# Attention feeding a two-level mixture of experts on one core: split weight loads, gate products moved to the end of a phase, and a rearranged start

## The chip, the cores and the metric

The kernel runs on one core of a Trainium2 chip. A core has five engines that run side by side[...]: TensorE (PE in the profile, with its weight loads as PEld) multiplies matrices, VectorE (DVE) and ScalarE (ACT) work on elements, GpSimd (POOL) [...]issues some of the transfers, SyncE (SP) issues the rest. TensorE writes its products to PSUM[...]. The metric is the device time of one execution in microseconds; lower is better.

## What is computed

Eight batches of multi-query attention (16 heads share one key and value head, 384 tokens, head size 64) are followed by a mixture of experts: 4 groups of 4 experts, each expert being two products of 1024 by 1024 with a ReLU between.

```python
scores = (q @ k.T) / 8                       # q: 8 x 16 x 384 x 64; k, v: 8 x 1 x 384 x 64
attn = softmax(scores)                       # over the keys
x = (attn @ v) -> (3072 tokens, 1024)        # heads side by side
g_idx = argmax(x @ w_group)                  # 4 groups
e_idx = argmax(x @ w_expert[g_idx])          # 4 experts in the group
combined = softmax weight of the group * softmax weight of the expert
out = combined * (relu(x @ w1[g_idx, e_idx]) @ w2[g_idx, e_idx])
```

All values are float32; w1 and w2 are 4 MB each for each of the 16 experts.

## The kernel before

It works through 24 *pieces* `p`, three pieces of 128 tokens for each batch. For one piece, `scores(p, j)` makes the scores of all heads against 64 keys (j = 0 to 5) and their exponentials; `pre_add`, `fold_keys`, `join` and `invert` build the sums over keys and their inverse; `values(p - 1, j)` multiplies the exponentials of the piece *before* by v; `weigh(p - 1)` divides and writes the result to `xT` (float32) on VectorE and to `xbf` (bf16) on GpSimd.

Most tokens of a batch choose the same expert, so the kernel counts the choices of the first 128 tokens of a batch, takes the most frequent expert, loads its two weight matrices and applies it to the whole batch. Pairs of a batch and an expert that this misses are done at the end. The work of one batch is 14 *units*: 8 `h_unit`s (first product and ReLU) and 6 `y_unit`s (second product). They are put into *phases* behind the attention of a piece, four or five at a time, so that TensorE always has work.

```python
def load_w1(w1, e):                       # two transfers, each with all 1024 columns of F
    for a in range(2):
        nc.gpsimd.dma_start(out=w1[a * D:(a + 1) * D], in_=w1f[bass.ds(e, 1), a]...)

def choose_b(b):                          # counts of the first 128 tokens, then the weight loads
    ps = side([P, GE], FP32, "c1ps")
    nc.tensor.matmul(out=ps[:], lhsT=ones_bf[:], rhs=first[b]..., start=True, stop=True)
    cnt = pool.tile([P, GE], FP32, tag="cnt1", bufs=1, name="cnt1")
    nc.vector.tensor_copy(out=cnt[:], in_=ps[:])
    nc.vector.max_with_indices(out_max=top[:], out_indices=idx[:], in_=cnt[:])
    reg = nc.values_load(idx[0:1, 0:1], engines=(ET.Pool,), ...)
    load_w1(w1, reg)
    nc.gpsimd.dma_start(out=w2[:], in_=w2f[bass.ds(reg, 1)]...)

def gate_c(b):                            # counts of the whole batch, and gsel, the y_units' scale
    ps = side([P, ST, GE], FP32, "cps")
    nc.tensor.matmul(out=ps[:]..., lhsT=ones_bf[:], rhs=ohe_t[b]..., start=True, stop=True)
    nc.vector.reduce_sum(out=cnt[:], in_=ps[:].rearrange("p s e -> p e s"), axis=AX)
    ...                                   # five more small VectorE operations, the last one writes gsel

def phase(n, jobs):
    for i in range(n):
        fill(1)                           # one unit, if the weights of its batch have been asked for
        some_q()                          # one transfer of a later q
        if i > 0 and jobs:
            jobs.pop(0)()
    while jobs:
        jobs.pop(0)()

def jobs_gates(b):                        # in the phase of each batch's second piece
    return [gate_a of b, gate_both(b), count_both(b)]     # cut: for b = 0 three smaller ones

FIVES = (9, 13, 17, 20)
for p in range(NP):
    b, st = divmod(p, ST)
    for j in range(3):
        scores(p, j)
    if p == 0:   prep_k(1)
    elif p == 1: turn_q(2, ...)           # q of piece 2 turned by TensorE, copied by ScalarE
    elif p == 2: turn_q(3, ...)
    elif p < NP - 1: prep_q(p + 1)        # q of the next piece turned by VectorE
    for j in range(KB):                   # KB = 6
        if jobs: jobs.pop(0)()
        if p > 0: values(p - 1, j)
        if j == 2 and p > 0: join(p - 1)
        if j + 3 < KB: scores(p, j + 3)
        if j > 0: pre_add(p, j)
        if j == 2 and p > 0: invert(p - 1)
        if j == 3: stats_q(p)
        ...
    if p > 0: weigh(p - 1)
    fold_keys(p)
    ...
    if p >= ST:                           # from piece 3 on
        phase(5 if p in FIVES else 4, jobs)
```

`gate_a` is the product of `xT` with the gate weights (ScalarE copies it to `part`), `gate_both` sums it up and lets VectorE find the maxima (`choose_a`, `gate_logits`, `gate_math`; its result `ohe` is the operand of the count products), `count_both` is `choose_b` and `gate_c`. All products but those of `values` rotate through three PSUM slots of two banks (`ps_s`, tag "s"); `values` has one slot of its own. The exponentials have nine buffers, `presum` one. Before the loop, q of pieces 0 and 1 are turned by TensorE. After the loop, the last units run between the small steps that find and do the pairs left over.

Of the kernel before, what the change touches and what calls it, by code (L numbers as in the profile page):

```python
# [9 lines left out]
FP32 = mybir.dt.float32  # L10
# [3 lines left out]
P = 128  # L14
ACTF = mybir.ActivationFunctionType
OP = mybir.AluOpType
AX = mybir.AxisListType.X
# [4 lines left out]
def kernel(  # L22
# [11 lines left out]
    nc = tc.nc  # L34
    B, H, S, D = q.shape
# [37 lines left out]
    def side(shape, dtype, name):  # L73
        return ps_s.tile(shape, dtype, tag="s", name=name)
# [20 lines left out]
    def some_q(n=1):  # L95
        for _ in range(n):
            if q_todo:
                q_todo.pop(0)()
# [38 lines left out]
            q_nat.append(qe)  # L137

    def load_w1(w1, e):
        for a in range(2):  # L140
            nc.gpsimd.dma_start(out=w1[a * D:(a + 1) * D], in_=w1f[bass.ds(e, 1), a].rearrange("e p k f -> (e p) k f"))  # L141

    ones_bf = singles.tile([P, P], BF16, name="ones_bf")
    nc.vector.memset(ones_bf[:], 1.0)
# [72 lines left out]
    def turn_q(p, nat, copies):  # L217
        qT[p] = pool.tile([P, 2 * CW], FP32, tag="qT", bufs=2, name="qT")
        n = HP // len(copies)
        for i, copy in enumerate(copies):  # L220
            ps = side([P, 2 * CW], FP32, "qps")
            for h in range(n):
                nc.tensor.transpose(out=ps[:, h * P:(h + 1) * P], in_=nat(i * n + h).rearrange("p a d -> p (a d)"), identity=ident[:])
            copy(out=qT[p][:, i * n * P:(i + 1) * n * P], in_=ps[:, 0:n * P])
# [78 lines left out]
    def gate_a(b, lo, hi):  # L303
        n = (hi - lo) * P
        ps = side([P, CW], FP32, "gps")
        for r in range(2):
            for j in range(4):
                ko = 4 * r + j
                nc.tensor.matmul(out=ps[32 * j:32 * j + 32, 0:n], lhsT=gw[:, ko, :], rhs=xT[b][:, ko, lo * P:hi * P], start=(r == 0), stop=(r == 1), tile_position=(0, 32 * j))
        part[b] = part_all  # L310
        nc.scalar.copy(out=part[b][:, lo * P:hi * P], in_=ps[:, 0:n])

    def gate_b(b, lo=0, hi=ST):
        ps = side([P, ST, 32], FP32, "lps")
        for st in range(lo, hi):
            nc.tensor.matmul(out=ps[:, st, :], lhsT=part[b][:, st * P:(st + 1) * P], rhs=sel[:], start=True, stop=True)  # L316
        return ps
# [3 lines left out]
    def choose_a(b, ps):  # L321
        gate_logits(b, ps, 0, 1)
        L = logits[b][:, 0]
        mx = pool.tile([P, 5], FP32, tag="mx1", bufs=1, name="mx1")
        nc.vector.reduce_max(out=mx[:], in_=L, axis=AX)
        oh = pool.tile([P, 5, 4], FP32, tag="oh1", bufs=1, name="oh1")
        nc.vector.tensor_tensor(out=oh[:], in0=L, in1=mx[:].unsqueeze(2).to_broadcast([P, 5, 4]), op=OP.is_ge)
        ohe = pool.tile([P, 4, 4], BF16, tag="ohe1", bufs=1, name="ohe1")
        nc.vector.tensor_mul(out=ohe[:], in0=oh[:, 1:5, :], in1=oh[:, 0, :].unsqueeze(2).to_broadcast([P, 4, 4]))
        first[b] = ohe  # L330

    def choose_b(b):
        ps = side([P, GE], FP32, "c1ps")
        nc.tensor.matmul(out=ps[:], lhsT=ones_bf[:], rhs=first[b][:].rearrange("p g e -> p (g e)"), start=True, stop=True)
        cnt = pool.tile([P, GE], FP32, tag="cnt1", bufs=1, name="cnt1")
        nc.vector.tensor_copy(out=cnt[:], in_=ps[:])
        top = pool.tile([P, 8], FP32, tag="top", bufs=1, name="top")
        idx = pool.tile([P, 8], U32, tag="idx", bufs=2, name="idx")
        nc.vector.max_with_indices(out_max=top[:], out_indices=idx[:], in_=cnt[:])
        reg = nc.values_load(idx[0:1, 0:1], engines=(ET.Pool,), min_val=0, max_val=GE - 1, skip_runtime_bounds_check_because="an index into 16 counts")  # L340
        w1 = wpool.tile([P, KO, F], BF16, tag="w1", name="w1")
        load_w1(w1, reg)
        w2 = wpool.tile([P, FO, Dm], BF16, tag="w2", name="w2")
        nc.gpsimd.dma_start(out=w2[:], in_=w2f[bass.ds(reg, 1)].rearrange("a p k f -> (a p) k f"))
        wts[b] = (w1, w2)
        choice[b] = idx
# [26 lines left out]
        gv = gate_all[:, b * GE:(b + 1) * GE, :].rearrange("p (g e) s -> p s g e", g=G)  # L373
        nc.vector.tensor_mul(out=gv, in0=ohe[:], in1=tt[:].unsqueeze(3).to_broadcast([P, ST, 4, 4]))

    def gate_c(b):
        ps = side([P, ST, GE], FP32, "cps")
        nc.tensor.matmul(out=ps[:].rearrange("p s e -> p (s e)"), lhsT=ones_bf[:], rhs=ohe_t[b][:].rearrange("p s g e -> p (s g e)"), start=True, stop=True)
        cnt = pool.tile([P, GE], FP32, tag="cnt", bufs=1, name="cnt")
        nc.vector.reduce_sum(out=cnt[:], in_=ps[:].rearrange("p s e -> p e s"), axis=AX)  # L380
        idf = pool.tile([P, 1], FP32, tag="idf", bufs=1, name="idf")
        nc.vector.tensor_copy(out=idf[:], in_=choice[b][:, 0:1])
        mask = pool.tile([P, GE], FP32, tag="mask", bufs=1, name="mask")
        nc.vector.tensor_scalar(out=mask[:], in0=iota16[:], scalar1=idf[:, 0:1], scalar2=None, op0=OP.is_equal)
        nc.vector.scalar_tensor_tensor(out=extra[:, b * GE:(b + 1) * GE], in0=cnt[:], scalar=0.0, in1=mask[:], op0=OP.is_gt, op1=OP.subtract)
        gm = pool.tile([P, ST, GE], FP32, tag="gm", bufs=1, name="gm")
        nc.vector.tensor_mul(out=gm[:], in0=gate_all[:, b * GE:(b + 1) * GE, :].rearrange("p e s -> p s e"), in1=mask[:].unsqueeze(1).to_broadcast([P, ST, GE]))
        gs = pool.tile([P, ST], FP32, tag="gsel", bufs=4, name="gsel")
        nc.vector.reduce_sum(out=gs[:], in_=gm[:], axis=AX)  # L389
        gsel[b] = gs  # L390
# [47 lines left out]
    stats_k(0)  # L438
    turn_k_first()
    turn_q(0, lambda h: q_raw[0][:, 0, h], [nc.scalar.copy, nc.vector.tensor_copy])  # L440
    turn_q(1, lambda h: q_raw[0][:, 1, h], [nc.vector.tensor_copy])
    load_gw()

    units = []
# [2 lines left out]
    def fill(n):  # L447
        while n > 0:
            if not units:
                if begun[0] >= B or begun[0] not in wts:  # L450
                    return
                units.extend(first_units(begun[0]))
                begun[0] += 1
            units.pop(0)()
            n -= 1

    def phase(n, jobs):
        for i in range(n):
            fill(1)
            some_q()  # L460
            if i > 0 and jobs:
                jobs.pop(0)()
        while jobs:
            jobs.pop(0)()

    def gate_both(b):
        ps = gate_b(b)
        choose_a(b, ps)
        gate_logits(b - 1, ps, 1, ST)
        gate_math(b - 1)  # L470

    def count_both(b):
        choose_b(b)
        gate_c(b - 1)

    def jobs_gates(b):
        if b == 0:
            return [lambda: gate_a(0, 0, 1), lambda: choose_a(0, gate_b(0, 0, 1)), lambda: choose_b(0)]
        return [lambda: gate_a(b, 0, ST), lambda: gate_both(b), lambda: count_both(b)]

    bound = {}
    oki = singles.tile([1, 1], I32, name="oki")
# [17 lines left out]
        nc.vector.tensor_copy(out=oki[:], in_=okf[:])  # L500
        bound["okf"] = okf

    FIVES = (9, 13, 17, 20)
    for p in range(NP):
        b, st = divmod(p, ST)
        jobs = jobs_gates(0) if p == 2 else []
        if st == 0 and b + 1 < B:
            load_q(b + 1)
        for j in range(3):
            scores(p, j)  # L510
        if p == 0:
            prep_k(1)
        elif p == 1:
            turn_q(2, lambda h: q_raw[0][:, 2, h], [nc.scalar.copy])
        elif p == 2:
            turn_q(3, lambda h: q_nat[h // HC][:, h % HC], [nc.scalar.copy])
        elif p < NP - 1:
            prep_q(p + 1)
        for j in range(KB):
            if jobs:  # L520
                jobs.pop(0)()
            if p > 0:
                values(p - 1, j)
            if j == 2 and p > 0:
                join(p - 1)
            if j + 3 < KB:
                scores(p, j + 3)
            if j > 0:
                pre_add(p, j)
            if j == 2 and p > 0:  # L530
                invert(p - 1)
            if j == 3:
                stats_q(p)
            if p < 4 and 0 < j < 5:
                some_q()
        assert not jobs
        if p > 0:
            weigh(p - 1)
        fold_keys(p)
        if st == 1 and b + 1 < B:  # L540
            if b > 0:
                load_k(b + 1)
            load_v(b + 1)
        if st == 2 and b + 1 < B:
            if b > 0:
                prep_k(b + 1)
            stats_k(b + 1)
        if p >= ST:
            jobs = []
            if st == 1:  # L550
                jobs = jobs_gates(b)
            if p == NP - 1:
                jobs = [bound_a, bound_b]
            phase(5 if p in FIVES else 4, jobs)

    done[0] = True
    join(NP - 1)
# [8 lines left out]
    gate_logits(last, gate_b(last, 1, ST), 1, ST)  # L566
    gate_math(last)
    fill(1)
    gate_c(last)
    fill(1)  # L570
    pe = side([P, CW], FP32, "pe")
    nc.tensor.matmul(out=pe[:, 0:1], lhsT=extra[0:1, :], rhs=one[0:1, 0:1], start=True, stop=True)
# [238 lines left out]
```

## Time and profile before

| What | Value |
|---|---|
| Time, median of three executions | 493.03 us (492.92 to 494.19) |
| Span of the profiled execution | 491.4 us |
| Mean granted TensorE clock | 0.993 |
| DVE busy | 307.9 us (63%) |
| ACT busy | 247.8 us (50%) |
| POOL busy | 48.0 us (10%) |
| Exponentials on ACT (144) | 142.1 us |
| Score products on PE | 141.9 us |
| Value products on PE | 140.6 us |
| First and second expert products on PE | 90.9 and 86.7 us |
| Weights of one batch: two transfers for w1, one for w2 | 12.9 and 23.9 us to landing |

Busy times of different engines overlap and do not add up to the span. In the timeline each line is a run of like instructions with its start and length; the bracket gives the idle time of that engine just before it, and what is taken to have ended it. A wait for several semaphores is put down to the last one that the profile shows, so the name in the bracket is at times that of an engine which had long been done.

### The profile page before, as it was taken

Reading aid. Unit: us, or ns where it says so; the run is one execution under the profiler, and the core shown is the slowest. Engines: PE = TensorE matmul, PEld = TensorE weight load, DVE = VectorE, ACT = ScalarE, POOL = GpSimd, SP = SyncE. Lnnn points to the kernel's source line nnn. Section 1 sums busy time; section 2 is a strip of 40 time slices with the busy share of each in tenths; the row PEclk is TensorE's granted clock in tenths of the full one; section 3 lists DMA queues with packets and bytes.
Section 4 is the critical chain, followed back from the end, with each engine's and each line's share of the span. In section 5 each row is a group of like instructions: output and inputs, shape, how many; then the busy total and the mean of one; then the engine's idle time right before and its main releaser. Section 6 shows DMA issues by size and latency. Waiting matters only on the chain. (4 is left out here: it accounts for less than half of the span.)

```text
span 491.4 us, 9357 instructions
## 1 busy us (share of the span) xinstructions
PE 466.2 (95%) x3828; PEld 202.7 (41%) x3828; DVE 307.9 (63%) x487; ACT 247.8 (50%) x346; POOL 48.0 (10%) x64
## 2 busy tenths in 40 slices
PE   7999698999999998999999999999999999999993
PEld 6333244333344334434434334433434434445651
DVE  4779737856777847866677756855686675734200
ACT  2966263664456463565456464565465455423231
POOL 1002000200010000200010002000010002001000
PEclk9999899999999999999999999999999999999998
DMA  8797992996949595996789386977599303985990
GB/s 161 93 118 130 218 187 36 158 245 169 126 66 213 135 222 65 154 211 175 129 119 208 106 187 114 192 146 187 120 155 209 119 21 102 200 190 150 238 261 29
DMA packets 146242, 74.52 MB, mean 152 GB/s; under 512 B 120443, under 2 KB 120443, under 8 KB 146192
## 3 DMA queue, kind: packets, MB, share of 16 engines
q0 software_dynamic: 19008, 37.84, 42.6%
q1 hardware_dynamic: 126384, 35.81, 36.0%
q8 instruction: 32, 0.52, 0.4%
q10 hardware_dynamic: 800, 0.20, 0.2%
q14 instruction: 18, 0.15, 0.1%
HBM read 92.62 MB, written 19.40 MB: 228 GB/s over the span
## 5 line engine op out<-in xcount | busy, mean ns | idle before, releaser
L248 ACT ACTIVATE pt<-s 128x1024 f32<-128x1024 f32 x144 | 142.1, 1026 | 69.7 <-PE s L246 68.5
L246 PE MATMUL s<-qT,kT 64*64 64x512 f32 x1152 | 141.9, 595 | 2.3 <-ACT hT L402 1.7
L285 PE MATMUL o<-pt,v 64*64 64x512 f32 x1152 | 140.6, 590 | 1.2 <-DVE xT L296 1.2
L256 DVE TENSOR_TENSOR presum<-presum,pt 128x1024 f32<-128x1024 f32 x96 | 116.6, 1215 | 7.9 <-DVE presum L254 0.5
L401 PE MATMUL hps<-xbf,w 128*128 128x384 bf16 x512 | 90.9, 330 | 5.4 <-POOL xbf L297 5.0
L409 PE MATMUL yps<-w,hT 128*128 128x512 bf16 x384 | 86.7, 379 | 0.0
L285 PEld LDWEIGHTS o<-pt,v 64*64 64x64 f32 x1152 | 43.4, 133 | 78.7 <-issue 74.9
L401 PEld LDWEIGHTS <-w 128*128 128x128 bf16 x512 | 49.1, 100 | 50.3 <-issue 21.5
L254 DVE TENSOR_TENSOR presum<-pt 128x1024 f32<-128x1024 f32 x24 | 29.1, 1214 | 61.2 <-ACT pt L248 61.1
L402 ACT ACTIVATE hT<-hps 128x384 bf16<-128x384 f32 x64 | 31.3, 489 | 71.2 <-PE hps L401 71.1
L246 PEld LDWEIGHTS s<-qT,kT 64*64 64x64 f32 x1152 | 39.8, 133 | 63.6 <-issue 51.4
L297 POOL CAST xbf<-xT 128x1024 bf16<-128x1024 f32 x24 | 25.0, 1042 | 332.9 <-DVE xT L296 332.9
L409 PEld LDWEIGHTS <-hT 128*128 128x128 bf16 x384 | 36.3, 98 | 49.3 <-issue 8.9
L410 ACT ACTIVATE y<-yps,gsel 128x512 f32<-128x512 f32 x36 | 24.8, 688 | 48.9 <-PE yps L409 41.8
L296 DVE TENSOR_TENSOR xT<-o,rinv 128x1024 f32<-128x1024 f32 x24 | 29.2, 1218 | 3.6 <-PE o L285 3.6
L275 DVE STREAM_TRANSPOSE rinv<-rc 128x1024 f32<-128x1024 f32 x24 | 29.9, 1246 | 0.8
L260 DVE TRANSPOSE_TENSOR_REDUCE fold<-presum 128x32 f32<-128x1024 f32 x24 | 29.6, 1235 | 0.0
L273 DVE RECIPROCAL rc<-sm 128x32 f32<-128x32 f32 x24 | 8.6, 358 | 29.6 <-PE sm L268 29.5
L238 DVE STREAM_TRANSPOSE qT<-qraw 128x1024 f32<-128x1024 f32 x20 | 24.3, 1215 | 2.0 <-DMA qraw<-in_q_dram 1.7
L204 ACT ACTIVATE junk<-qraw 128x1024 bf16<-128x1024 f32 x21 | 22.0, 1049 | 0.0
L141 POOL DMA_DIRECT2D w<-in_moe_w_dram x18 | 12.6, 706 | 69.8 <-DVE gsel L389 43.5
L351 DVE COPY L<-lps 128x20 f32<-128x20 f32 (+1 forms) x16 | 3.0, 186 | 25.5 <-PE lps L316 25.5
(147 smaller groups left out, 187.9 us busy)
## 6 DMA issues: line engine op xcount, KB each, us to landing
w<-in_moe_w_dram POOLq DMA_DIRECT2D x18, 1024.0 KB, 12.9
w<-in_moe_w_dram POOLq DMA_DIRECT2D x9, 2048.0 KB, 23.9
qraw<-in_q_dram SPq DMA_DIRECT2D x56, 192.0 KB, 5.0
out_dram<-y SPq DMA_DIRECT2D x36, 256.0 KB, 4.4
x_bf<-xbf SPq DMA_DIRECT2D x8, 768.0 KB, 3.7
out_dram<-yt SPq DMA_DIRECT2D x12, 256.0 KB, 6.1
v<-in_v_dram SPq DMA_DIRECT2D x16, 96.0 KB, 2.6
k<-in_k_dram SPq DMA_DIRECT2D x28, 48.0 KB, 3.3
```

The lines of the kernel that those rows point to most:

```text
L246: nc.tensor.matmul(out=ps[64 * c:64 * c + 64, a, :], lhsT=kT[b][r, j * D:(j + 1) * D], rhs=qT[p][r, c * CW:(c + 1) * CW], start=True, stop ...
L248: nc.scalar.activation(out=t[:], in_=ps[:], func=ACTF.Exp, scale=scale)
L254: nc.vector.tensor_add(out=presum[p][:], in0=pt[p, 0][:], in1=pt[p, 1][:])
L256: nc.vector.tensor_add(out=presum[p][:], in0=presum[p][:], in1=pt[p, j][:])
L260: nc.vector.tensor_reduce(out=fold[p][:], in_=presum[p][:].rearrange("p a (n i) -> p (a n) i", i=32), axis=AX, op=OP.add, apply_transpose= ...
L275: nc.vector.transpose(out=t[:].rearrange("p (b i) -> p b i", i=32), in_=rc[:].rearrange("p c b -> p (c b)").unsqueeze(2).to_broadcast([P, ...
L285: nc.tensor.matmul(out=o_ps[p][64 * a:64 * a + 64, c, :], lhsT=v_sb[b][r, j, :], rhs=pt[p, j][r, a, :], start=(j == 0), stop=(j == KB - 1))
L296: nc.vector.tensor_mul(out=xT[b][:, :, ts], in0=o_ps[p][:].rearrange("p c (h n) -> p (c h) n", n=P), in1=rinv[p][:].rearrange("p (h n) -> ...
L297: nc.gpsimd.tensor_copy(out=xbf[b][:, :, ts], in_=xT[b][:, :, ts])
L401: nc.tensor.matmul(out=ps[:, 0:S], lhsT=w1[:, ko, fc * P:(fc + 1) * P], rhs=xb[:, ko, :], start=(ko == 0), stop=(ko == KO - 1))
L402: nc.scalar.activation(out=state["h"][:, fc, :], in_=ps[:, 0:S], func=ACTF.Relu)
L409: nc.tensor.matmul(out=ps[:], lhsT=state["h"][:, fo, st * P:(st + 1) * P], rhs=w2[:, fo, nh * CW:(nh + 1) * CW], start=(fo == 0), stop=(fo ...
```

## The change

The change reorders work and splits transfers; the products computed stay the same.

1. **Weights by halves of F.** w1 is loaded in four transfers instead of two, the first 512 columns first, so that the first four `h_unit`s need only the first half.
2. **Start.** The turn of q for piece 1 goes behind the first scores of piece 0. The turns for pieces 2 and 3 move from before the values loop of pieces 1 and 2 to its fourth step.
3. **Sums earlier.** `pre_add` for j = 1 and 2 stands ahead of the values loop, the others at j = 1 to 3 instead of 3 to 5.
4. **First units inside block 4.** The phase of piece 3 is dropped. Piece 4 does three units between its first three scores and the values of piece 3. `FIVES` is rearranged; the number of units by the end of the loop stays 88.
5. **Gate products last in a phase.** `gate_a` stands behind the last but one unit of a phase, `gate_both` behind the last one.
6. **Counts together.** The two count products go one piece later, into one PSUM slot; ScalarE copies both with one instruction, and VectorE reads the copy.

```diff
     def load_w1(w1, e):
-        for a in range(2):
-            nc.gpsimd.dma_start(out=w1[a * D:(a + 1) * D], in_=w1f[bass.ds(e, 1), a]...)
+        for c in range(2):
+            fs = slice(c * F // 2, (c + 1) * F // 2)
+            for a in range(2):
+                nc.gpsimd.dma_start(out=w1[a * D:(a + 1) * D, :, fs], in_=w1f[bass.ds(e, 1), a, :, :, fs]...)
...
+    def counts(now, full):
+        n = GE * (1 + ST)
+        ps = side([P, n], FP32, "cps")
+        lo, hi = (0 if now is not None else GE), (n if full is not None else GE)
+        ...                                  # one product for `now`, one for `full`
+        t = pool.tile([P, n], FP32, tag="cnt1", bufs=1, name="cnt1")
+        nc.scalar.copy(out=t[:, lo:hi], in_=ps[:, lo:hi])
+        ...                                  # choose_b(now, t[:, 0:GE]); gate_c(full, t[:, GE:n])
...
     turn_q(0, ...)
-    turn_q(1, ...)
...
-        return [lambda: gate_a(b, 0, ST), lambda: gate_both(b), lambda: count_both(b)]
+        return [lambda: gate_a(b, 0, ST), lambda: gate_both(b)]
...
-    FIVES = (9, 13, 17, 20)
+    FIVES = (8, 12, 16, 20, 22)
...
         for j in range(3):
             scores(p, j)
+            if p == 0 and j == 0:
+                turn_q(1, ...)
         if p == 0:
             prep_k(1)
-        elif p == 1:
-            turn_q(2, ...)
-        elif p == 2:
-            turn_q(3, ...)
-        elif p < NP - 1:
+        elif 2 < p < NP - 1:
             prep_q(p + 1)
+        if jobs:
+            jobs.pop(0)()
+        if p == ST + 1:
+            fill(3)
+        for j in (1, 2):
+            pre_add(p, j)
         for j in range(KB):
-            if jobs:
-                jobs.pop(0)()
             if p > 0:
                 values(p - 1, j)
...
-            if j > 0:
-                pre_add(p, j)
+            if 0 < j < 4:
+                pre_add(p, j + 2)
             if j == 2 and p > 0:
                 invert(p - 1)
             if j == 3:
                 stats_q(p)
+                if p == 1:
+                    turn_q(2, ...)
+                elif p == 2:
+                    turn_q(3, ...)
+            if jobs:
+                jobs.pop(0)()
...
-        if p >= ST:
-            jobs = []
+        if p > ST:
+            n = 5 if p in FIVES else 4
+            steps = {}
+            if st == 2 and b > 0:
+                steps = {0 if b == 1 else 1: lambda: counts(b, b - 1)}
             if st == 1:
-                jobs = jobs_gates(b)
+                gate_a_, gate_b_ = jobs_gates(b)
+                steps = {n - 2: gate_a_, n - 1: gate_b_}
+                if b == B - 1:
+                    steps = {1: gate_a_, 2: gate_b_, n - 1: lambda: counts(b, b - 1)}
             if p == NP - 1:
-                jobs = [bound_a, bound_b]
-            phase(5 if p in FIVES else 4, jobs)
+                steps = {1: bound_a, 2: bound_b}
+            for i in range(n):
+                fill(1)
+                some_q()
+                if i in steps:
+                    steps[i]()
...
-    gate_c(last)
+    counts(None, last)
```

More of the change, by code (lines that the diff above doesn't have):

```diff
@@ L139, in load_w1 @@
     def load_w1(w1, e):
-        for a in range(2):
-            nc.gpsimd.dma_start(out=w1[a * D:(a + 1) * D], in_=w1f[bass.ds(e, 1), a].rearrange("e p k f -> (e p) k f"))
+        for c in range(2):
+            fs = slice(c * F // 2, (c + 1) * F // 2)
+            for a in range(2):
+                nc.gpsimd.dma_start(out=w1[a * D:(a + 1) * D, :, fs], in_=w1f[bass.ds(e, 1), a, :, :, fs].rearrange("e p k f -> (e p) k f"))
     ones_bf = singles.tile([P, P], BF16, name="ones_bf")
@@ L330, in choose_a, with choose_b @@
         first[b] = ohe
[L332 to L336, printed above, removed]
+    def counts(now, full):
+        n = GE * (1 + ST)
+        ps = side([P, n], FP32, "cps")
+        lo, hi = (0 if now is not None else GE), (n if full is not None else GE)
+        if now is not None:
+            nc.tensor.matmul(out=ps[:, 0:GE], lhsT=ones_bf[:], rhs=first[now][:].rearrange("p g e -> p (g e)"), start=True, stop=True)
+        if full is not None:
+            nc.tensor.matmul(out=ps[:, GE:n], lhsT=ones_bf[:], rhs=ohe_t[full][:].rearrange("p s g e -> p (s g e)"), start=True, stop=True)
+        t = pool.tile([P, n], FP32, tag="cnt1", bufs=1, name="cnt1")
+        nc.scalar.copy(out=t[:, lo:hi], in_=ps[:, lo:hi])
+        if now is not None:
+            choose_b(now, t[:, 0:GE])
+        if full is not None:
+            gate_c(full, t[:, GE:n])
+    def choose_b(b, cnt):
         top = pool.tile([P, 8], FP32, tag="top", bufs=1, name="top")
         idx = pool.tile([P, 8], U32, tag="idx", bufs=2, name="idx")
-        nc.vector.max_with_indices(out_max=top[:], out_indices=idx[:], in_=cnt[:])
+        nc.vector.max_with_indices(out_max=top[:], out_indices=idx[:], in_=cnt)
         reg = nc.values_load(idx[0:1, 0:1], engines=(ET.Pool,), min_val=0, max_val=GE - 1, skip_runtime_bounds_check_because="an index into 16 counts")
@@ L374, in gate_math, with gate_c @@
         nc.vector.tensor_mul(out=gv, in0=ohe[:], in1=tt[:].unsqueeze(3).to_broadcast([P, ST, 4, 4]))
-    def gate_c(b):
-        ps = side([P, ST, GE], FP32, "cps")
-        nc.tensor.matmul(out=ps[:].rearrange("p s e -> p (s e)"), lhsT=ones_bf[:], rhs=ohe_t[b][:].rearrange("p s g e -> p (s g e)"), start=True, stop=True)
+    def gate_c(b, per):
         cnt = pool.tile([P, GE], FP32, tag="cnt", bufs=1, name="cnt")
-        nc.vector.reduce_sum(out=cnt[:], in_=ps[:].rearrange("p s e -> p e s"), axis=AX)
+        nc.vector.reduce_sum(out=cnt[:], in_=per.rearrange("p (s e) -> p e s", s=ST), axis=AX)
         idf = pool.tile([P, 1], FP32, tag="idf", bufs=1, name="idf")
@@ L440 @@
     turn_q(0, lambda h: q_raw[0][:, 0, h], [nc.scalar.copy, nc.vector.tensor_copy])
-    turn_q(1, lambda h: q_raw[0][:, 1, h], [nc.vector.tensor_copy])
     load_gw()
@@ L455, in fill @@
             n -= 1
[L457 to L461, printed above, removed]
-                jobs.pop(0)()
-        while jobs:
-            jobs.pop(0)()
     def gate_both(b):
@@ L470, in gate_both @@
         gate_math(b - 1)
-    def count_both(b):
-        choose_b(b)
-        gate_c(b - 1)
     def jobs_gates(b):
         if b == 0:
-            return [lambda: gate_a(0, 0, 1), lambda: choose_a(0, gate_b(0, 0, 1)), lambda: choose_b(0)]
-        return [lambda: gate_a(b, 0, ST), lambda: gate_both(b), lambda: count_both(b)]
+            return [lambda: gate_a(0, 0, 1), lambda: choose_a(0, gate_b(0, 0, 1)), lambda: counts(0, None)]
+        return [lambda: gate_a(b, 0, ST), lambda: gate_both(b)]
     bound = {}
@@ L510 @@
             scores(p, j)
+            if p == 0 and j == 0:
+                turn_q(1, lambda h: q_raw[0][:, 1, h], [nc.vector.tensor_copy])
         if p == 0:
             prep_k(1)
-        elif p == 1:
-            turn_q(2, lambda h: q_raw[0][:, 2, h], [nc.scalar.copy])
-        elif p == 2:
-            turn_q(3, lambda h: q_nat[h // HC][:, h % HC], [nc.scalar.copy])
-        elif p < NP - 1:
-            prep_q(p + 1)
+        elif 2 < p < NP - 1:
+            prep_q(p + 1)
+        if jobs:
[4 more added lines that the diff above has]
+            pre_add(p, j)
         for j in range(KB):
-            if jobs:
-                jobs.pop(0)()
             if p > 0:
@@ L533 @@
                 stats_q(p)
-            if p < 4 and 0 < j < 5:
+                if p == 1:
+                    turn_q(2, lambda h: q_raw[0][:, 2, h], [nc.scalar.copy])
+                elif p == 2:
+                    turn_q(3, lambda h: q_nat[h // HC][:, h % HC], [nc.scalar.copy])
+            if jobs:
+                jobs.pop(0)()
+            if p <= ST and 0 < j < 5:
                 some_q()
```

## The prediction, made before the changed kernel ran

> **What bounds the kernel now.** I read the busy times of the page first, then TensorE's waits, then the timelines around each wait.
>
> ```profile
> PE 466.2 (95%) x3828; PEld 202.7 (41%) x3828; DVE 307.9 (63%) x487; ACT 247.8 (50%) x346; POOL 48.0 (10%) x64
> ```
>
> TensorE is busy for 466.2 of 491.4 us, and the change takes no product away. So only its idle 25 us, and products that ran at a lower clock, can be won. Of the 25, about 8 lie behind the last product at 483.6 us, 1.3 ahead of the first.
>
> ```profile
> PE hps L401 <- POOL xbf L297: 5.0, 2, 4.3
> PE cps L378 <- DVE ohe L365: 2.8, 6, 0.5
> PE s L246 <- ACT hT L402: 1.7, 5, 0.3
> PE gps L309 <- ACT hT L402: 1.7, 3, 0.6
> PE qps L223 <- DMA qn<-in_q_dram: 1.2, 1, 1.2
> PE o L285 <- DVE xT L296: 1.2, 1, 1.2
> PE qps L223 <- ACT pt L248: 0.8, 1, 0.8
> PE s L246 <- ACT y L410: 0.6, 1, 0.6
> PE pq L493 <- DVE sq L487: 0.5, 1, 0.5
> ```
>
> Columns: total us, times, longest. With 0.3 more for hps these waits are 15.8; reading every idle stretch over 0.1 us off the timeline I get 16.0. They fall in two kinds. Up to 66 us: 1.19 at 8.0, 0.80 at 18.2, 1.19 at 43.6, 4.29 at 52.8, together 7.47. After it: the gates, once a batch, and two single ones, together 8.5. TensorE's timeline shows one of each kind:
>
> ```profile
> 57.12 7.04 PE L401 MATMUL hps<-xbf,w 128*128 128x384 bf16 x32 [4.29 <-POOL xbf L297]
> ...
> 74.67 2.77 PE L401 MATMUL hps<-xbf,w 128*128 128x384 bf16 x16
> 78.01 1.50 PE L309 MATMUL gps<-xT,gw 128*32 128x384 f32 x16 [0.57 <-ACT hT L402]
> ...
> 83.28 0.20 PE L378 MATMUL cps<-ohe,ones_bf 128*128 128x48 bf16 x1 [0.47 <-DVE ohe L365]
> 83.82 2.81 PE L246 MATMUL s<-qT,kT 64*64 64x512 f32 x24 [0.35 <-ACT hT L402]
> ```
>
> The first line holds a second loss: 32 products took 7.04 us, 16 of the same took 2.77, so some 1.5 us went to a lower clock after the idle stretch. The windows view (PE, PEld, DVE, ACT, POOL, granted clock, DMA) has it as 0.76:
>
> ```profile
> 57.00:64.20 7.20, 7.08 (x36) 3.68 (x39) 1.24 (x2) 1.48 (x4) 0.07 (x1) 0.76 1.27 207
> ```
>
> What is behind the 4.29 us is VectorE. Its timeline:
>
> ```profile
> 50.98 3.84 DVE L256 TENSOR_TENSOR presum<-presum,pt 128x1024 f32<-128x1024 f32 x3
> 54.74 1.22 DVE L296 TENSOR_TENSOR xT<-o,rinv 128x1024 f32<-128x1024 f32 x1
> 55.88 1.24 DVE L260 TRANSPOSE_TENSOR_REDUCE fold<-presum 128x32 f32<-128x1024 f32 x1
> ```
>
> The values of piece 2 were ready at 52.8, but VectorE still added exponentials until 54.7, then weighed, and GpSimd's cast to bf16 ran from 56.02 to 57.06. The first unit started at 57.12. The weights were not the cause: w1's second half of partitions landed at 52.7 by the semaphore's times. The same lag of VectorE is at the second kind: weigh(3) ran 76.65 to 77.9, and gate_a, put down to ACT, started at 78.01.
>
> [...] The trace has no w1 split by columns; it shows the transfers of one batch following each other[...].
>
> **The start (parts 2, 3, 4).** Scores of piece 0 need only the first turn, copied at about 8.8. They start near 8.3 and wait for the second copy, the second turn follows at 9.3 when its q has landed. First scores then end near 9.4 rather than 11.2, but the exponential for j = 1, which VectorE's first add waits for, comes only behind the turn: it ends near 12.3 against 13.3. From there VectorE has no pause in my walk. Adds are 1.27 us apart, invert 1.56, weigh 1.13, fold 1.2, prep_q 1.13, the gate steps of batch 0 together 1.4 with waits (all start to start in its timeline). Piece 0: 5 adds and fold, 7.8, to 20.1. Piece 1: 5 adds, invert, weigh, fold, 10.2, to 30.3. Piece 2: the same and the gate steps, 11.7, to 42.0. Piece 3: prep_q, 5 adds, invert, weigh, 10.2, to 52.2. Cast: 53.3, against 57.06.
>
> TensorE in the same walk: piece 1 ends near 26.4, piece 2 near 39.5 (before, 40.8), scores of piece 3 to 42.1, no wait for weigh(1), which ends at 40.9; values of piece 2 end at 50.2 against 52.83. Scores of piece 4 need nothing new and go to 52.7. A wait of 0.6 for the cast, under the length that lowered the clock, then three units at 1.35 until 57.4. Before, with four units, the same point was 64.09 + 2.63 = 66.7; a fourth unit at 1.35 makes it 65.4 at like work. **Gain 8.0**, which is 7.47 + 1.5 less about 1.0 of small new waits.
>
> **The weights (part 1).** choose_b comes some 1.9 us earlier; four columns-by-partition quarters land at about 5.5 us for each half. First columns are there near 45, well ahead of 53. On POOL four issues of 0.69 take 1.4 us more a batch, beside everything. In the steady part the load starts a piece later, about 14 us after the old moment, but the units of that batch begin 22 us or more after that. Worth by itself: 0 to 0.3 us.
>
> **The gates (parts 3, 5, 6).** Walking one piece from the start of its scores: joins come at 7.2, so before, invert at 7.2 pushed three adds behind it and weigh ended at 13.7; now only the last add is behind it, and weigh ends near 12.3, with values ending at 10.4. gate_a stands two units later still, so 0.57 goes. Counts are asked for a piece after ohe exists, so 0.47 goes, and 0.35 ahead of the scores with them. The stretches for batches 1 to 7 are 1.39, 1.37, 1.39, 0.96, 0.81, 0.80, 0.58: 7.3 us. The others are 0.73 at 115.6 (a unit waiting for xbf) and 0.48 (bound_b behind a late VectorE); both get the 1.4 us of an earlier weigh. **Gain 8.5 at most.** The counts' copy on ACT costs 8 times about 0.2 us on an engine that is half idle: nothing.
>
> **What I take off.** gate_both right ahead of the scores makes ACT wait for dl (about 1.6 us) before the next exponential; that one then ends 2.9 us after gate_b, and its slot is needed at 3.5. Margins of half a us will not all hold. At the end, the last w2 landed at 478.0 and its products began at 479.98; the split w1 goes ahead of it in the queue, and 2 us of room may shrink to 1. I take 1.5 us off for these. Sum: 8.0 + 8.5 - 1.5 = 15.0, so 493.0 - 15.0 = **478.0 us**.
>
> **The rivals.**
> First, *the wait moves*: VectorE, busy 11.65 of 12.0 us up to 57, remains the limit at the start, and any pause in it (a late exponential, the count's copy now behind two exponentials on ACT) goes straight into the cast. For it speaks that my walk leaves it no slack; against it, that a delay of the cast by 2 us costs just 2. If the start gives 5 instead of 8[...]: 482 to 483.
> Second, *gates merely displaced*: the chain part, gate_b, dl, ex now stands against the next exponentials, and VectorE starts its adds 3 us later in each third piece; kT of the next batch is then done near 32.9 on a clock where its scores start at 33.9. If 0.7 us a batch returns: 483.
> Third, *transfers*: 2 KB rows instead of 4 KB and loads that overlap other q transfers; q took 20.9 us to land beside the weights at 36 to 64 us. If the end waits for w2, or a prep_q for q: 2 to 4 us, 480 to 482.
>
> **Range and chances.** Each alone leaves a gain over 2% (under 483.2) or just at it; two together lose it. The most that can be won is 16.0 + 1.5, 475.5. So the range is 475.5 to 483.5, faster by over 2% at 0.87, within 2% at 0.11, slower 0.02, the last for a stall that I do not see at all.
>
> **What would show it.** Right: no stretch over 1 us ahead of the first unit, that unit near 53, clock 1.0 throughout to the end; no wait of cps on ohe nor of gate_a; VectorE without pause from 12 to 52. Wrong: hps waiting for xbf by 2 us or more, scores waiting in each third piece for an exponential or for kT, py waiting for the last weights, or PE busy time itself changed.

## The result and the profile after

The changed kernel takes 497.16 us (median of four, 495.48 to 497.63) against 492.98 in the same comparison: 1.0074 times as long, 95% interval 1.0045 to 1.0103. A gain of 15 us was predicted; it lost 4.

The page's busy line, and then the waits of TensorE (line, what it waited for, total us, times, longest), of the changed kernel:

```profile
PE 467.5 (94%) x3810; PEld 203.9 (41%) x3828; DVE 304.4 (61%) x479; ACT 248.0 (50%) x355; POOL 60.3 (12%) x82
```

```profile
PE s L248 <- DVE top L352: 12.0, 4, 4.6
PE s L248 <- ACT y L421: 3.9, 2, 2.9
...
PE hps L412 <- POOL xbf L299: 0.6, 1, 0.6
```

The old waits are gone: cps on ohe, gps on VectorE's weigh, 4.3 us on xbf (now 0.6). New ones stand in their place. The scores wait 12.0 us in four places, put down to `top`, VectorE's maximum of the counts. `top` is no operand of the scores. What VectorE does just ahead of it is `kT` of the next batch, which is. VectorE's timeline around the longest of the four, in the third piece of batch 3:

```profile
186.32 0.22 DVE L387 TENSOR_TENSOR gate_all<-ohe,tt 128x48 f32<-128x48 bf16 x1
193.11 1.25 DVE L240 STREAM_TRANSPOSE qT<-qraw 128x1024 f32<-128x1024 f32 x1 [6.57 <-DMA qraw<-in_q_dram]
...
204.32 0.54 DVE L230 STREAM_TRANSPOSE kT<-k 128x384 f32<-128x384 f32 x1
204.78 0.14 DVE L352 MAX8 top<-cnt 128x8 f32<-128x16 f32 x1
```

The cause is one line up from where the wait shows. VectorE idled 6.57 us for q of the next batch, then did its sums without a pause and came to kT at 204.32; TensorE's scores started at 204.91, after 4.62 us of idling. The 3.9 us put to `y` are partly the same lateness: before one of these waits, ScalarE stood 6.3 us for `gsel`, VectorE's last count step, and before the other 5.0 us for a y store to leave its buffer. VectorE's turns of q wait for q's transfers for 22.6 us in five places, in four of them (batches 2, 3, 5 and 6) for 3.5 to 6.6 us; before the change it was 1.7 us in two. SyncE's queue shows why q was late (start, length):

```profile
162.41 0.46 SPq L89 DMA_DIRECT2D qraw<-in_q_dram  x1
162.96 10.08 SPq L442 DMA_DIRECT2D out_dram<-y  x1
173.09 0.43 SPq L89 DMA_DIRECT2D qraw<-in_q_dram  x1
...
184.90 3.89 SPq L89 DMA_DIRECT2D qraw<-in_q_dram  x4
```

Issuing one y store took 10.08 us, behind the first q transfer, and everything after it in that queue moved back. Ahead of q the queue held the 768 KB of `x_bf` and a y store too, both beside the weights; q's first rows moved at 170.4. So the last four q transfers were issued from 184.90 on, where VectorE wanted them at 186.5. The weights of batch 2 were asked for at 148.1 and moving until 177.3. Before the change they were asked for at 141.0, had landed at about 167 and only then, at 171.3, came the first q transfer of that stage; no SyncE issue after 70 us took over 3 us. The same two transfers before the change:

```profile
171.31 0.86 SPq L89 DMA_DIRECT2D qraw<-in_q_dram  x1
172.27 1.76 SPq L431 DMA_DIRECT2D out_dram<-y  x1
```

The transfers in two windows of the changed kernel show what it means for q to share with weights (packets, MB, share of the window). From 172 to 176 us both are under way, from 188 to 191 q is alone:

```profile
q0 software_dynamic: 373, 0.74, 97.2%
q1 hardware_dynamic: 884, 0.12, 25.9%
```

```profile
q1 hardware_dynamic: 3191, 0.40, 160.9%
```

q0 carries the weights, q1 mainly q. Beside the weights, 884 packets of q1 in 4 us, 221 in a microsecond; alone, 3191 in 3 us, 1064. A q transfer has 1536 rows of 128 bytes. At the first rate that is 7 us, at the second 1.4 (an estimate from these two windows). In the first window q1 had 884 of 1257 packets but 0.12 of 0.86 MB; what shares the time out between the two queues was not shown.

### The profile page after: what moved, and what is told of

Read it like the earlier page. It is cut to its first block, busy times and chain, and to the rows that moved or that the text cites. A ratio compares the mean times of both kernels' runs of the same rounds, so it can differ in the third digit from the quotient of the medians.

```text
span 495.7 us, 9385 instructions
## 1 busy us (share of the span) xinstructions
PE 467.5 (94%) x3810; PEld 203.9 (41%) x3828; DVE 304.4 (61%) x479; ACT 248.0 (50%) x355; POOL 60.3 (12%) x82
## 5 line engine op out<-in xcount | busy, mean ns | idle before, releaser
L248 PE MATMUL s<-qT,kT 64*64 64x512 f32 x1152 | 146.7, 609 | 16.2 <-DVE top L352 12.0
L287 PE MATMUL o<-pt,v 64*64 64x512 f32 x1152 | 142.1, 594 | 0.0
L412 PE MATMUL hps<-xbf,w 128*128 128x384 bf16 x512 | 89.0, 326 | 2.2 <-ACT hT L413 1.6
L420 PE MATMUL yps<-w,hT 128*128 128x512 bf16 x367 | 85.6, 379 | 0.9
L248 PEld LDWEIGHTS s<-qT,kT 64*64 64x64 f32 x1152 | 40.8, 135 | 79.9 <-issue 52.9
L240 DVE STREAM_TRANSPOSE qT<-qraw 128x1024 f32<-128x1024 f32 x20 | 24.5, 1225 | 22.6 <-DMA qraw<-in_q_dram 22.6
L143 POOL DMA_DIRECT2D w<-in_moe_w_dram x36 | 24.8, 707 | 41.9 <-DVE gsel L400 22.0
L421 ACT ACTIVATE yt<-yps,gsel 128x512 f32<-128x512 f32 x12 | 8.2, 687 | 15.6 <-PE yps L420 12.0
```

Of the source, the lines that this page charges most:

```text
L248: nc.tensor.matmul(out=ps[64 * c:64 * c + 64, a, :], lhsT=kT[b][r, j * D:(j + 1) * D], rhs=qT[p][r, c * CW:(c + 1) * CW], start=True, stop ...
L287: nc.tensor.matmul(out=o_ps[p][64 * a:64 * a + 64, c, :], lhsT=v_sb[b][r, j, :], rhs=pt[p, j][r, a, :], start=(j == 0), stop=(j == KB - 1))
L412: nc.tensor.matmul(out=ps[:, 0:S], lhsT=w1[:, ko, fc * P:(fc + 1) * P], rhs=xb[:, ko, :], start=(ko == 0), stop=(ko == KO - 1))
L420: nc.tensor.matmul(out=ps[:], lhsT=state["h"][:, fo, st * P:(st + 1) * P], rhs=w2[:, fo, nh * CW:(nh + 1) * CW], start=(fo == 0), stop=(fo ...
L421: nc.scalar.activation(out=y, in_=ps[:], func=ACTF.Copy, scale=gs_of()[:, st:st + 1])
```

## The experiments

All against the kernel before in the same comparison. Theory 1: the weights, asked for a piece later (part 6), lie over the q transfers and y stores of the next batch, and late q makes VectorE late. Theory 2: VectorE itself has too much in the third piece. Theory 3: the halves of w1 disturb the other transfers.

**Counts in the phase.**

```diff
-                steps = {0 if b == 1 else 1: lambda: counts(b, b - 1)}
+                steps = {}
...
-                steps = {n - 2: gate_a_, n - 1: gate_b_}
-                if b == B - 1:
-                    steps = {1: gate_a_, 2: gate_b_, n - 1: lambda: counts(b, b - 1)}
+                steps = {1: gate_a_, 2: gate_b_, n - 1: lambda: counts(b, b - 1)}
```

> The changed kernel, but for every batch gate_a, gate_both and both counts stand in the phase of its second piece, after units 2, 3 and the last, as they did before the change; the weights are then asked for about 13 us earlier. Theory 1 (weights asked for a piece later stream while the next batch's q pieces and y stores are queued on SyncE; q comes late, VectorE's turn of q waits for it, and kT and the scores wait for VectorE): the four late turns of q no longer wait (22.6 us before VectorE's turns falls under 3), no SyncE issue over 5 us after 70 us, no stretch over 1 us on TensorE after the first unit, and the waits of cps (0.5 a batch) are back: 483 to 485. Theory 2 (VectorE has too much in each third piece, since the gate steps now stand ahead of its sums and the six count steps behind them; q plays no part): also better, about 484, so this run does not part these two. Theory 3 (the halves of w1 disturb the other transfers): stays above 493.

Measured: 476.46 us, 0.9662 times before (0.9646 to 0.9678). Turns of q wait 3.5 us, a little over the 3 expected. With the gates, the counts and so the request for the weights back in the phase of the second piece, the 4 us of loss become a gain of 16. That is better than the 483 to 485 expected: one gate wait stays, the cps one, 1.8 us in four batches.

**Choice in the phase, whole count later.**

```diff
-                steps = {0 if b == 1 else 1: lambda: counts(b, b - 1)}
+                steps = {0 if b == 1 else 1: lambda: counts(None, b - 1)}
...
-                steps = {n - 2: gate_a_, n - 1: gate_b_}
+                steps = {n - 3: gate_a_, n - 2: gate_b_, n - 1: lambda: counts(b, None)}
```

> The changed kernel, but the choice of the expert (count of the first 128 tokens, and the weight loads) stands at the end of the phase of the second piece, gate_a and gate_both one unit earlier each, and only the count of the whole batch before stays a piece later. Theory 1: weights start as early as before the change, no late q, and the waits of cps are gone as well: 478 to 480. Theory 2: the gate steps leave the third piece, the count steps stay in it: some waits of the scores on VectorE stay, 481 to 486. Theory 3: above 490.

Measured: 477.1 us, 0.9678 (0.9662 to 0.9694). As theory 1 has it, if a little faster; not to be told from the run before it. Turns of q wait 5.1 us in three places, but no scores wait for VectorE. Six count steps left in VectorE's third piece cost nothing that can be seen.

**q in long rows.** This run leaves the late weights and all VectorE work as they are and changes only how q is read.

```diff
-...rearrange("p h k d -> p (h k) d"), in_=qv[b, a, j, :, hs].rearrange("i h k d -> i (h k) d")
+...rearrange("p h k d -> p (h k d)"), in_=q[b].rearrange("h s d -> (h s d)").rearrange("(c i r) -> c i r", c=8, i=32)[4 * i + 2 * a + j]
```

> The changed kernel, but from batch 1 on q is read in rows of 6 KB that lie together, instead of rows of 128 bytes: the same bytes and the same number of transfers, but the wrong elements of q in each place, so the output isn't the reference's; the experts chosen stay the same. Everything else, the late weights too, is as in the changed kernel. Theory 1: q lands in a few us even beside the weights, VectorE's turns wait under 2 us in all, SyncE is not held up, and the scores do not wait: 477 to 481. Theory 2: kT is late in the third pieces as before, 493 to 497. Theory 3: between, as the y stores are still held up, 485 to 495.

Measured: 477.52 us, 0.9694 (0.9673 to 0.9715). Weights are asked for as late in the order of work as in the changed kernel. The turns of q wait 1.8 us in three places, and the y store that took 10.08 us is issued in 0.34 behind a q transfer of 32 rows:

```profile
  DMA qraw<-in_q_dram: 1.8, 3
```

```profile
158.40 0.39 SPq L89 DMA_DIRECT2D qraw<-in_q_dram  x1
158.95 0.34 SPq L442 DMA_DIRECT2D out_dram<-y  x1
```

Theory 2 falls: with every gate and count step in the same place VectorE is in time once q is. Long rows take away two things at once, q's small share beside the weights (0.12 of 0.86 MB in the changed kernel's window) and the hold-up of SyncE's issues; no run parts these two. One stretch of 2.7 us remains, at 216.8, where scores wait for an eviction of y; the y stores are slow beside the weights even so (median 8.4 us to landing, 4.4 before the change).

**w1 whole.**

```diff
-        for c in range(2):
-            fs = slice(c * F // 2, (c + 1) * F // 2)
-            for a in range(2):
-                nc.gpsimd.dma_start(out=w1[a * D:(a + 1) * D, :, fs], in_=...)
+        for a in range(2):
+            nc.gpsimd.dma_start(out=w1[a * D:(a + 1) * D], in_=...)
```

> The changed kernel with w1 in two transfers of whole rows, as before the change. Theory 1: q is as late or later[...]: 497 to 501. Theory 2: no difference within 1 us but for the first unit. Theory 3: the loss is gone, under 485.

Measured: 498.7 us, 1.0119 (1.0097 to 1.0141); turns of q wait 22.4 us. Theory 3 falls: the halves don't make the loss. Whether they ease it by 1 us is not settled, the interval touches that of the changed kernel.

**Late counts alone.** The kernel before, with part 6 only.

```diff
-        return [gate_a, gate_both, count_both]
+        return [gate_a, gate_both]
...
+            if st == 2 and 0 < b < B - 1:
+                if b == 1:
+                    counts(b, b - 1)
+                else:
+                    jobs = [lambda: counts(b, b - 1)]
```

> The kernel before the change with one part of it alone: both counts, and with them the request for the weights, go into the phase of the third piece, in one PSUM slot copied by ScalarE; gates, sums, start and w1's two transfers stay as before. Theory 1 (late weights against q and the y stores): the waits of cps go (about 5 us won), but q is late in several third pieces and some 20 us are lost, as between the changed kernel and the run with long rows of q: 503 to 513. Theory 2 (VectorE overloaded by gate steps ahead of the sums): gates stay in mid phase here, so nothing is lost, 487 to 493.

Measured: 508.02 us, 1.0307 (1.029 to 1.0325), the middle of what theory 1 gave. The part that does the harm does it alone: turns of q wait 29.8 us in five places.

**Start and sums alone.** The kernel before with parts 2, 3 and 4. Against the changed kernel:

```diff
-                steps = {0 if b == 1 else 1: lambda: counts(b, b - 1)}
+                steps = {}
...
-                steps = {n - 2: gate_a_, n - 1: gate_b_}
-                if b == B - 1:
-                    steps = {1: gate_a_, 2: gate_b_, n - 1: lambda: counts(b, b - 1)}
+                steps = {1: gate_a_, 2: gate_b_, 3: lambda: count_both(b)}
```

(`count_both`, `choose_b` and `gate_c` as before the change, w1 whole.)

> The kernel before with the start, the earlier sums and the units inside block 4 alone; gate products, counts as two products with VectorE's copy, the request for the weights and w1's two transfers stay as before. As the prediction had it, the start is worth 8.0 and gate waits other than the 0.57 ahead of gate_a remain (0.47 and 0.35 a batch): 481 to 485. The rival, which the run with counts in the phase suggests: earlier sums alone take most of the gate waits with them: 477 to 480. In both, no late q.

Measured: 481.69 us, 0.9765 (0.9749 to 0.9782). The prediction's version of it holds, not the rival: in five of seven batches the waits behind the counts stay.

```profile
PE cps L378 <- DVE ohe L365: 2.3, 5, 0.5
PE s L246 <- ACT hT L402: 1.4, 4, 0.3
```

**Counts in the phase, w1 whole.** As the first run, with w1 as in the run "w1 whole".

> The run with counts in the phase (476.5), but w1 in two transfers of whole rows. If halves matter only where the first unit waits for weights, nothing changes: 475.5 to 477.5, since GpSimd's cast and not w1 is what the first unit waits for. If halves bring the first unit forward: 478 to 480, with an idle stretch of 2 us or more before it.

Measured: 477.48 us, 0.9684 (0.967 to 0.97). With halves it was 0.9662 in another comparison; at most 1 us, and the first unit waits the same 0.62 us for the cast in both. From the run with start and sums alone it differs by one slot and one ScalarE copy for both counts, which in the phases of five units also stand one unit later. It is 4.2 us faster; TensorE waits 0.46 in each of four batches instead of 0.58 to 0.81 in each of seven, which makes 3.4 of it.

**Counts mid-piece.**

```diff
+        if st == 2 and 0 < b < B - 1:
+            jobs = [lambda: None, lambda: counts(b, b - 1)]
...
-                steps = {0 if b == 1 else 1: lambda: counts(b, b - 1)}
+                steps = {}
```

> The changed kernel with both counts in the third piece after its first values, not behind the units: the weights are asked for some 14 us sooner than in the changed kernel, some 7 us later than in the run with counts in the phase. Theory 1 (overlap of weights with q and stores): the overlap is mostly gone, VectorE's turns wait for q under 8 us in all (22.6 in the changed kernel): 477 to 483. Theory 2: six count steps now even stand between the sums of the third piece, VectorE is as late as in the changed kernel: over 488.

Measured: 475.77 us, 0.9646 (0.963 to 0.9662), the fastest median of all and a little under the 477 expected at least; its interval overlaps that of the first run. Turns of q wait 1.9 us. TensorE's only idle stretches over 0.25 us after its first product are 0.43, 0.62, and at the end 0.59, where py waits for the last weights.

**Counts at the end of the attention.** `[lambda: None] * 5` ahead of the counts in the same edit.

> The changed kernel with both counts in the third piece after its last values and ahead of its first unit: later than in the mid-piece run (475.8), a little sooner than in the changed kernel (497.2), where VectorE also turns kT ahead of the count steps. Theory 1: the weights begin some 4 to 8 us sooner than in the changed kernel, so they lie over fewer q transfers; the turns of q wait between the two runs, 5 to 20 us in all, and the time lies between: 480 to 494. If it is as fast as the mid-piece run, a few us of overlap cost nothing; if it is as slow as the changed kernel, any overlap with the first q transfers is enough.

Measured: 487.43 us, 0.9886 (0.9866 to 0.9906); turns of q wait 10.8 us. Between the neighbours in both numbers, as theory 1 asks. In order of when the weights of batch 2 are asked for (133.9, 144.2 and 148.1 us), the three runs with counts in the third piece are mid-piece, end of attention and the changed kernel: 475.8, 487.4 and 497.2 us. Here the counts stand ahead of kT, and the waits of the scores are put down to kT itself:

```profile
PE s L248 <- DVE kT L230: 6.5, 3, 4.3
```

**q held back.** The collision avoided from the other side.

```diff
                 fill(1)
-                some_q()
+                some_q(2 if st == 1 else 0)
```

> The changed kernel with its late weights, but q of the next batch is asked for only in the phase of each second piece, two transfers a unit, and none in the phases of the first and third pieces, so that the weights are mostly in. Theory 1 (the two streams must not lie over each other, lateness of the weights itself costs nothing): y stores are no longer held up behind q, SyncE has no issue over 5 us in the phases of first pieces; q is asked for later but lands faster, VectorE's turns wait under 12 us in all: 477 to 487. If late weights themselves were the cost, or if asking for q a piece later costs as much as the overlap: over 490.

Measured: 508.88 us, 1.0325 (1.0303 to 1.0347). A miss. No y store took over 5 us to issue, as theory 1 said, but one transfer of k took 6.25, and in batches 2 to 6 VectorE waits 5.2 to 6.5 us for q. In batch 3 it turned q at 194.71 after 5.93 us of waiting:

```profile
180.18 10.32 SPq L89 DMA_DIRECT2D qraw<-in_q_dram  x8
```

Eight q transfers in a row take 10.3 us to issue even here, where the weights were in by then (an estimate from the changed kernel, where they moved until 177.3), so asked for in one phase they end too late. This corrects theory 1: what costs is q landing after VectorE wants it, whatever delays it; the weights lying over it are the cause in the changed kernel, and holding q back is another.

## Why the prediction was wrong, by its own steps

- **What bounds the kernel, and how much can be won: right.** TensorE's waits were the thing to win. With q out of the way (long rows) the time is 477.5, predicted 478.0. That they come so close is partly luck: the 2.7 us for y were not foreseen, and the 1.5 taken off hardly showed.
- **The start, 8.0: right, a little high.** The first unit began at 54.1 (53.3 predicted) after 0.62 us of waiting (0.6), and the clock did not drop there (1.00 from 54.1 to 60.0 us). At the prediction's own point of comparison, after the first three units, TensorE was at 58.1 (57.4 predicted) against 65.4: 7.3 us. At piece 5's scores the lead is 10.3 us (73.56 against 83.82), but with one unit and the counts less done.
- **The gates, 8.5 at most: right in sum, partly in cause.** At piece 8 the changed kernel was 12.8 us ahead with one unit less done; the long-rows run ends with its last product 15.0 ahead, the mid-piece run 16.2. The 0.57 ahead of gate_a is gone in every run with the earlier sums, so it was weigh. The 0.35 ahead of the scores was given to counting later; counts in the phase lose it too, with the one slot and ScalarE's copy. Gate products last in the phase are not needed: the first run has them in the middle, and its interval overlaps that of the fastest.
- **The weights, "0 to 0.3 us": the step that failed.** It asked if weights arrive in time for their own units. They do: no unit waits for them. It did not ask what their transfers, some 26 us a batch, lie over once they start a piece later. The third rival named the q transfers, quoted 20.9 us for one beside the weights, and still gave it 2 to 4 us, a size for one wait, while q came 3.5 to 6.6 us late in four batches. Measured between the changed kernel and the long-rows run: last products at 488.62 and 468.59, 20.0 apart. Of these 14.8 are idle stretches (18.8 against 4.0) and 5.1 a lowered clock after two of them. The trace before had shown the collision once, at its start, where four q transfers beside the weights of batch 0 kept SyncE busy for 24 us:

```profile
40.57 24.21 SPq L89 DMA_DIRECT2D qraw<-in_q_dram  x4
```

- **The second rival, VectorE late for kT: the place was right, the reason not.** kT is where TensorE waits, but only because q came late; the margin of 1 us that the prediction gave it held in the long-rows run (in batch 3, kT done at 194.50, scores at 195.52).
- **What I took off, 1.5: too much.** The mid-piece run's last product is 16.2 us ahead (467.40 against 483.6), 0.3 under the 16.5 of start and gates. Its gates stand last in the phase, and no exponential behind them held the scores up; at the end w2 is waited for by 0.59 us.

The windows view of the changed kernel has the lowered clock (the third number from the end, ahead of DMA share and GB/s):

```profile
203.00:212.00 9.00, 7.09 (x40) 2.24 (x44) 6.01 (x15) 3.08 (x3) 4.66 (x6) 0.62 0.51 71
231.00:236.00 5.00, 3.94 (x24) 1.32 (x28) 2.03 (x2) 3.54 (x4) 0.00 (x0) 0.66 1.23 256
```

9.00 times 0.38 and 5.00 times 0.34 are the 5.1 us.

## What to carry to other kernels

When a large transfer is moved, ask what it will lie over and not only if it arrives in time: here the weights of a batch, early enough for their own use, cost 20 us through short-row transfers in another queue. A wait named after an instruction that is no operand is read one step back along that engine, to the last instruction that *is* one and to what delayed it. And a change of several parts is worth taking apart: the rest of this one is a gain of some 16 us, one part hid it.

## What the runs showed of the hardware that was not expected

- The time to issue a y store went with the transfers around it: one took 10.08 us to issue on SyncE behind a single q transfer of 1536 rows, while the weights streamed from another queue. Behind a q transfer of 32 rows, beside the same weights, it took 0.34.
- The drop of the TensorE clock did not go by the length of one idle stretch. In the run with q held back, two stretches of 3.31 us began at 327.1 and 386.4. Over ten microseconds with each, PE is busy for the same 6.69 us, and the granted clock was 0.83 with the first and 1.00 with the second:

```profile
327.00:337.00 10.00, 6.69 (x49) 2.40 (x52) 7.51 (x16) 3.93 (x5) 4.65 (x6) 0.83 0.39 57
386.00:396.00 10.00, 6.69 (x63) 2.79 (x64) 8.89 (x17) 4.39 (x6) 4.65 (x6) 1.00 0.37 53
```

In the run with late counts alone, a stretch of 2.02 us at 385.7 went with a granted clock of 0.83 (384 to 394 us); in the changed kernel, one of 3.09 us at 376.6 went with 1.00 (376 to 386 us). What decides it was not shown.
